# Taking the units of a fused FFT and feed-forward kernel in pairs: two first products, then two second products bank by bank

## The chip, the core and the metric

The kernel runs on one core of a Trainium2 chip. The metric is the device time of one execution in microseconds (us); three executions of the kernel before took 1721.28, 1721.38 and 1722.38 us, the median is 1721.38 us. The core has TensorE (PE, with its weight loads listed apart as PEld), VectorE (DVE), ScalarE (ACT), GpSimd (POOL) and SyncE (SP), which issues the DMAs. Each engine takes its instructions in the order in which they stand in its own list and waits for the others by semaphores.

## What is computed

```python
def _attn_ref(x):                       # x: 8 x 3008 x 256
    X = np.fft.fft(x, axis=1)
    X = np.fft.fft(X, axis=2)
    return X.real.astype(np.float32)

def _moe_ref(x, w_in, w_out):           # x: 24064 x 256, w_in: 256 x 2048, w_out: 2048 x 256
    h = x @ w_in
    g = np.where(h >= 1, h, np.where(h <= -1, 0.0, (h + 1) ** 2 / 4))
    return (g @ w_out).astype(np.float32)

def reference(x, moe_w_in, moe_w_out):
    return _moe_ref(_attn_ref(x).reshape(8 * 3008, 256), moe_w_in, moe_w_out)
```

The real part of a two-dimensional FFT of each of the 8 batches goes through a feed-forward layer of 2048 hidden channels with a smooth step between its two matrix products.

## The kernel before

The FFT of a batch is made by matmuls in 15 pieces: eight pieces of stage 1 (`s1`, L301, copied out by ACT at L322 into `z`), one for the Nyquist row (`ny`, L329, copied out by ACT at L333 as `nyt`), and six of stage 2 (`s2`, L367, split at L186 on ACT and L188 on DVE into a high and a low part, `pqh` and `pql`). The second FFT axis is folded into `w_in`. All these pieces share one PSUM bank, tag `fft`.

The feed-forward part is cut into **units**. A unit is one batch, one of three chunks of its columns (482, 512 and 512 wide) and 128 of the 2048 hidden channels, so there are 8 x 3 x 16 = 384 units, and 16 units in a row add up into the same output. A unit runs through these steps, which the document calls by the short names given here:

- the **first product** (`gemm1`, L418): two PSUM banks, called .0 and .1 here, three matmuls each. The banks come from a ring of three, tag `uv`; a bank is free again when DVE has read it.
- **us** (L433, DVE) reads bank .0; **h0** and **h1** (L441 and L442, DVE) read bank .1 and make the two halves of `h`.
- **relu** (L447, ACT) and **square** (L451, ACT) make `a` from `h`, one after the other on the same tile.
- **larger** (L462, DVE) joins `a` and `h`, both in SBUF.
- **gh** (L466, ACT) rounds `h` to the high part that TensorE multiplies by, and **gl** (L471, POOL, two instructions) forms the rest. Both have rings of four tiles, so the `gh` of a unit takes over the tile of the unit four before it, which must have been multiplied by then. `h` and `a` have rings of three.
- the **second product** (`gemm2`, L572): four PSUM banks `acc0` to `acc3`, three matmuls each (high by high, high by low, low by high), added up over the 16 units of an output. It comes four units later (`LAG`). After the last of the 16 units the four banks are copied out (**evicted**): for all batches but the first, bank 0 by DVE (L559) and banks 1 to 3 by ACT (L557), and two DMAs write them.

The first 48 units or so are written out by hand in a table of steps (`WRITTEN`). Behind it the loop at the end issues unit by unit: first product, activation, the FFT pieces that fall due (`PLAN`), and the second product of the unit four before. The last three units follow a hand-written list (`END`). A scheduler turns the loop's program into the engines' lists: it keeps dependences, but places each instruction by its own estimates, and evictions are given a higher priority (`EVICT_AHEAD`). So the order on ACT and DVE is not the order in the text.

Of the kernel before, what the change touches and what calls it, by code (L numbers as in the profile page):

```python
# [29 lines left out]
NCHUNK = 3  # L30
NFT = FF // P
LAG = 4
EVICT_AHEAD = 150

C_ORDER = [*range(1, 8), 0, *range(8, NC)]
# [87 lines left out]
N_FIXED = 3  # L123
# [5 lines left out]
def fft_ffn_kernel(ctx: ExitStack, tc: tile.TileContext, x, cst, w_in, w_out, out):  # L129
    nc = tc.nc  # L130
# [36 lines left out]
    woh = wts.tile([P, NFT, D], F32R, name="woh")  # L167
    wol = wts.tile([P, NFT, D], F32R, name="wol")
# [211 lines left out]
    def fft_pieces(b):  # L380
        pieces = []
        for q in range(XC):
            pieces.append(stage1(b, q))
        pieces.append(nyquist(b))
        for h in range(NC // 4):
            pieces.append(stage2(b, h))
        return pieces
# [5 lines left out]
    units = []  # L393
    for b in range(NB):
        visits = 1 if b else 2
# [6 lines left out]
    n_units = len(units)  # L402
    acts, outs = {}, {}

    def new_o(i):
        b, k, *_ = units[i]
        return [sb.tile([P, 2, CH], F32, tag="o", name=f"o_{i}_{dh}", bufs=2) for dh in range(2)]

    def gemm1(i):
        b, k, f, *_ = units[i]  # L410
        n = WIDTH[k]
        hi, lo = pq[b, k]
        cols = slice(f * P, (f + 1) * P)
        uv = acts[i] = []
        for m in range(2):
            t = ps.tile([P, CH], F32, tag="uv", name=f"uv_{i}_{m}", bufs=3)
            for j, (w, r) in enumerate(((wh, hi), (wl, hi), (wh, lo))):
                nc.tensor.matmul(t[:, :n], w[m][:, cols], r[:, m, :n], start=(j == 0), stop=(j == 2))  # L418
            uv.append(t[:, :n])
            yield  # L420
# [6 lines left out]
    def common(i):  # L427
        b, k, f, *_ = units[i]
        n = WIDTH[k]
        uv = acts[i]  # L430
        us = sb.tile([P, CH], F32, tag="us", name=f"us_{i}", bufs=2)[:, :n]
        d = delta[:, f : f + 1]
        fixed(i, nc.vector.scalar_tensor_tensor(us, nyb[b, k][:, :n], d, uv[0], op0=ALU.mult, op1=ALU.add), 2)  # L433
        acts[i] = us, uv

    def hidden(i):
        b, k, f, *_ = units[i]
        n = WIDTH[k]
        us, (_, v) = acts[i]
        h = sb.tile([P, 2, CH], F32, tag="h", name=f"h_{i}", bufs=3)[:, :, :n]  # L440
        fixed(i, nc.vector.tensor_tensor(h[:, 0], us, v, op=ALU.subtract), 2)  # L441
        fixed(i, nc.vector.tensor_tensor(h[:, 1], us, v, op=ALU.add), 2)  # L442
        acts[i] = h, sb.tile([P, 2, CH], F32, tag="a", name=f"a_{i}", bufs=3)[:, :, :n]

    def relu(i, sl=slice(0, 2)):
        h, a = acts[i]
        fixed(i, nc.scalar.activation(a[:, sl], h[:, sl], AF.Relu, bias=half, scale=0.5), 2)  # L447

    def square(i, sl=slice(0, 2)):
        _, a = acts[i]  # L450
        fixed(i, nc.scalar.activation(a[:, sl], a[:, sl], AF.Square), 2)  # L451

    def halves(i):
        b, k, *_ = units[i]
        n = WIDTH[k]
        return tuple(
            sb.tile([P, 2, CH], F32R, tag=tag, name=f"{tag}_{i}", bufs=4)[:, :, :n] for tag in ("gh", "gl")
        )

    def larger(i, sl=slice(0, 2)):  # L460
        h, a = acts[i]
        fixed(i, nc.vector.scalar_tensor_tensor(h[:, sl], a[:, sl], 1.0, h[:, sl], op0=ALU.min, op1=ALU.max))  # L462

    def high_half(i, gh, sl=slice(0, 2)):
        h, _ = acts[i]
        fixed(i, nc.scalar.activation(gh[:, sl], h[:, sl], AF.Copy))  # L466

    def low_half(i, gh, gl, sg):
        h, _ = acts[i]
        eng = nc.vector if (i - n_units, sg) in VECTOR_HALVES else nc.gpsimd  # L470
        fixed(i, eng.tensor_tensor(gl[:, sg], h[:, sg], gh[:, sg].bitcast(F32), op=ALU.subtract))  # L471

    def activate(i):
        common(i)
        yield
        hidden(i)
        yield
        relu(i)
        yield
        square(i)  # L480
        yield
        larger(i)
        yield
        gh, gl = halves(i)
        high_half(i, gh)
        yield
        low_half(i, gh, gl, 0)
        yield
        low_half(i, gh, gl, 1)
        acts[i] = gh, gl  # L490

    def finish_units():

        parts = {"a": slice(0, 1), "b": slice(1, 2)}
        g = {}
        for step in END.split():
            kind, at = step[0], step[1]
            i = n_units - N_FIXED + (N_FIXED - 1 if at in parts else int(at))
            sl = parts.get(at, slice(0, 2))
            if kind == "G":  # L500
                drain(gemm1(i))
            elif kind == "M":
                drain(gemm2(i - LAG))
            elif kind == "u":
                common(i)
            elif kind == "h":
                hidden(i)
            elif kind == "r":
                relu(i, sl)
            elif kind == "s":  # L510
                square(i, sl)
            elif kind == "x":
                larger(i, sl)
            else:
                if i not in g:
                    g[i] = halves(i)
                if kind == "g":
                    high_half(i, g[i][0], sl)
                else:
                    low_half(i, *g[i], int(step[2]))  # L520
        acts.update(g)
        for i in range(n_units - LAG, n_units):
            drain(gemm2(i))
# [3 lines left out]
    def drain(step):  # L527
        for _ in step or ():
            pass

    def gemm2(i):
        b, k, f, first, last, (v, visits) = units[i]
        n = WIDTH[k]
        gh, gl = acts.pop(i)
        if first:
            start = -k % 5 if b == NB - 1 else 0
            tags = [BANKS[(start + j) % 5] for j in range(4)]
            accs[:] = [ps.tile([P, CH], F32, tag=t, name=f"acc_{i}_{j}", bufs=1) for j, t in enumerate(tags)]
            if v:

                outs[k] = new_o(i)
                for dh in range(2):
                    nc.sync.dma_start(outs[k][dh][:, :, :n], parts[k][dh, :, :, :n])
        if last:
            o = outs.pop(k) if v else new_o(i)
        banks = [(dh, sg) for dh in range(2) for sg in range(2)]
        if i == n_units - 1:
            banks.sort(key=lambda bank: bank[::-1])

        def evict(dh, sg):  # L550
            acc = accs[dh * 2 + sg]
            dst = o[dh][:, sg, :n]
            with tc.high_priority(offset=EVICT_AHEAD):
                if v:
                    nc.vector.tensor_tensor(dst, acc[:, :n], dst, op=ALU.add)
                elif sg or b and dh:
                    nc.scalar.activation(dst, acc[:, :n], AF.Copy)  # L557
                else:
                    nc.vector.tensor_copy(dst, acc[:, :n])  # L559
            if i == n_units - 1:  # L560
                nc.sync.dma_start(out[b, k, dh, sg, :, :n], dst)
            if sg and v < visits - 1:
                nc.sync.dma_start(parts[k][dh, :, :, :n], o[dh][:, :, :n])
            elif sg and i < n_units - 1:
                nc.sync.dma_start(out[b, k, dh].rearrange("s p t -> p s t")[:, :, :n], o[dh][:, :, :n])

        later = f"M{i}" in written
        for dh, sg in banks:
            wc = slice(dh * P, (dh + 1) * P)
            acc = accs[dh * 2 + sg]  # L570
            for j, (w, g) in enumerate(((woh, gh), (wol, gh), (woh, gl))):
                nc.tensor.matmul(  # L572
                    acc[:, :n], w[:, f, wc], g[:, sg], start=(first and j == 0), stop=(last and j == 2)
                )
            if last and not later:
                evict(dh, sg)
        if last and later:
            for bank in banks:
                yield
                evict(*bank)  # L580
        yield
# [4 lines left out]
    def fill(n):  # L586
# [3 lines left out]
    first = [fft_pieces(b) for b in range(min(NB, 2))]  # L590
# [21 lines left out]
        "G": gemm1,  # L612
        "U": activate,
        "M": gemm2,
    }

# [12 lines left out]
    written = set(WRITTEN.split())  # L629

    plan = {}
# [13 lines left out]
        fill(N_WARM)  # L645
        run_steps(WRITTEN)

    for i in range(n_units - N_FIXED):
        if f"G{i}" not in written:
            drain(gemm1(i))  # L650
            drain(activate(i))
        for f in plan.get(i, ()):
            drain(f if hasattr(f, "send") else f())
        if i >= LAG and f"M{i-LAG}" not in written:
            drain(gemm2(i - LAG))
    finish_units()


# [53 lines left out]
```

## Time and profile before

| | before |
|---|---|
| median of three executions | 1721.38 us |
| span of the profiled execution | 1720.0 us |
| PE busy | 1708.5 us (99%), 7782 matmuls |
| DVE busy | 1384.2 us (80%) |
| ACT busy | 1355.9 us (79%) |
| POOL busy | 1197.4 us (70%) |
| second product, three groups of L572 | 606.5 + 601.8 + 595.3 us |
| first product, three groups of L418 | 305.9 + 301.3 + 298.6 us |

The profiled execution's own time from its first to its last instruction is 1720.0 us, 1.4 us below the median of the three. The busy time of PE counts pipelined matmuls that overlap, so it is read here by the distance from one matmul's start to the next one's. The granted clock of TensorE is full from end to end.

### The profile page before, as it was taken

Reading aid. Unit: us, or ns where it says so; the run is one execution under the profiler, and the core shown is the slowest. Engines: PE = TensorE matmul, PEld = TensorE weight load, DVE = VectorE, ACT = ScalarE, POOL = GpSimd, SP = SyncE. Lnnn points to the kernel's source line nnn. Section 1 sums busy time; section 2 is a strip of 40 time slices with the busy share of each in tenths; the row PEclk is TensorE's granted clock in tenths of the full one; section 3 lists DMA queues with packets and bytes.
Section 4 is the critical chain, followed back from the end, with each engine's and each line's share of the span. In section 5 each row is a group of like instructions: output and inputs, shape, how many; then the busy total and the mean of one; then the engine's idle time right before and its main releaser. Section 6 shows DMA issues by size and latency. Waiting matters only on the chain.

```text
span 1720.0 us, 21494 instructions
## 1 busy us (share of the span) xinstructions
PE 1708.5 (99%) x7782; PEld 1404.1 (82%) x7782; DVE 1384.2 (80%) x1683; ACT 1355.9 (79%) x1593; POOL 1197.4 (70%) x856
## 2 busy tenths in 40 slices
PE   9999999999999999999999999999999999999999
PEld 6878888888888888888888888888788888888776
DVE  6998888777888778887888778887788777888887
ACT  7878877878777877788877887778877788777776
POOL 3777766877667866768666786667766676766775
PEclk9999999999999999999999999999999999999999
DMA  6123320111001010011100111001100001000000
GB/s 234 48 74 119 101 70 25 52 37 53 19 7 60 28 53 25 10 51 38 44 25 10 51 46 35 26 10 60 50 21 26 10 24 43 1 25 24 1 26 25
DMA packets 33456, 72.44 MB, mean 42 GB/s; under 512 B 4547, under 2 KB 9667, under 8 KB 33350
## 3 DMA queue, kind: packets, MB, share of 16 engines
q1 hardware_dynamic: 33350, 71.07, 12.5%
q8 instruction: 61, 1.00, 0.3%
q14 instruction: 45, 0.37, 0.1%
HBM read 43.25 MB, written 27.81 MB: 41 GB/s over the span
## 4 chain that ended last, share of the span: by engine, by line
PE 75%; POOL 11%; issue 5%; ACT 4%; DVE 4%; DMA 0%; SPq 0%; POOLq 0%; ACTq 0%; DVEq 0%
PE acc L572 46%; PE uv L418 23%; POOL gl L471 9%; PE s L367 2%; PE s L301 2%; DVE h L462 2%; ACT gh L466 2%; ACT a L451 1%; POOL y L150 1%; ACT a L447 1%; DVE h L442 1%; DVE h L441 0%; DMA raw<-in_moe_w_in_dram 0%; DVE us L433 0%; PE wps L261 0%
## 5 line engine op out<-in xcount | busy, mean ns | idle before, releaser
L471 POOL TENSOR_TENSOR gl<-h,gh 128x512 fp32r<-128x512 f32 (+1 forms) x764 | 1094.6, 1456 | 487.8 <-ACT gh L466 441.4
L462 DVE SCALAR_TENSOR_TENSOR h<-a,h 128x1024 f32<-128x1024 f32 (+1 forms) x385 | 567.5, 1475 | 237.1 <-ACT a L451 236.6
L466 ACT ACTIVATE gh<-h 128x1024 fp32r<-128x1024 f32 (+1 forms) x385 | 400.6, 1041 | 310.4 <-DVE h L462 272.8
L572 PE MATMUL acc<-gh,woh 128*128 128x512 f32 (+1 forms) x1536 | 606.5, 395 | 0.0
L572 PE MATMUL acc<-gl,woh 128*128 128x512 f32 (+1 forms) x1536 | 601.8, 392 | 0.9 <-POOL gl L471 0.8
L572 PE MATMUL acc<-gh,wol 128*128 128x512 f32 (+1 forms) x1536 | 595.3, 388 | 0.0
L447 ACT ACTIVATE a<-h,half 128x1024 f32<-128x1024 f32 (+1 forms) x385 | 431.8, 1122 | 23.0 <-DVE h L442 20.1
L451 ACT ACTIVATE a<-a 128x1024 f32<-128x1024 f32 (+1 forms) x385 | 399.2, 1037 | 7.8
L572 PEld LDWEIGHTS acc<-gl,woh 128*128 128x128 f32 x1536 | 288.4, 188 | 62.6 <-POOL gl L471 1.9
L572 PEld LDWEIGHTS acc<-gh,wol 128*128 128x128 f32 x1536 | 289.2, 188 | 60.8 <-POOL wol L188 0.4
L572 PEld LDWEIGHTS acc<-gh,woh 128*128 128x128 f32 x1536 | 289.1, 188 | 55.9 <-DVE o L559 0.2
L441 DVE TENSOR_TENSOR h<-us,uv 128x512 f32<-128x512 f32 (+1 forms) x384 | 259.6, 676 | 64.4 <-POOL gl L471 23.6
L418 PE MATMUL uv<-pqh,wh 128*128 128x512 f32 (+1 forms) x768 | 305.9, 398 | 1.1 <-DVE h L442 0.9
L418 PE MATMUL uv<-pql,wh 128*128 128x512 f32 (+1 forms) x768 | 301.3, 392 | 0.0
L418 PE MATMUL uv<-pqh,wl 128*128 128x512 f32 (+1 forms) x768 | 298.6, 389 | 0.0
L433 DVE SCALAR_TENSOR_TENSOR us<-nyb,delta,uv 128x512 f32<-128x512 f32 (+1 forms) x384 | 278.7, 726 | 5.1 <-PE uv L418 4.5
L442 DVE TENSOR_TENSOR h<-us,uv 128x512 f32<-128x512 f32 (+1 forms) x384 | 256.2, 667 | 0.0
L418 PEld LDWEIGHTS uv<-pqh,wh 128*128 128x128 f32 x768 | 144.3, 188 | 38.8 <-DVE h L442 6.8
L418 PEld LDWEIGHTS uv<-pql,wh 128*128 128x128 f32 x768 | 144.3, 188 | 31.9
L418 PEld LDWEIGHTS uv<-pqh,wl 128*128 128x128 f32 x768 | 144.2, 188 | 31.0 <-issue 1.2
L322 ACT ACTIVATE z<-s 64x192 f32<-64x192 f32 x244 | 82.6, 339 | 4.4 <-PE s L301 0.7
L150 POOL TENSOR_TENSOR y<-x 128x384 f32<-128x384 f32 x56 | 80.7, 1443 | 0.7 <-PE s L301 0.7
(59 smaller groups left out, 493.8 us busy)
## 6 DMA issues: line engine op xcount, KB each, us to landing
x<-in_x_dram SPq DMA_DIRECT2D x64, 384.0 KB, 3.1
out_dram<-o SPq DMA_DIRECT2D x30, 512.0 KB, 3.2
out_dram<-o SPq DMA_DIRECT2D x16, 482.0 KB, 3.3
nyb<-nyr SPq DMA_DIRECT2D x23, 256.0 KB, 5.6
raw<-in_moe_w_in_dram SPq DMA_DIRECT2D x8, 512.0 KB, 8.5
raw<-in_moe_w_out_dram SPq DMA_DIRECT2D x8, 512.0 KB, 4.5
part<-o SPq DMA_DIRECT2D x4, 512.0 KB, 2.6
o<-part SPq DMA_DIRECT2D x4, 512.0 KB, 3.5
```

The source lines that it names most:

```text
L150: nc.gpsimd.tensor_tensor(y, t[:, 0], t[:, 1], op=ALU.add)
L322: nc.scalar.activation(dst, src, AF.Copy)
L418: nc.tensor.matmul(t[:, :n], w[m][:, cols], r[:, m, :n], start=(j == 0), stop=(j == 2))
L433: fixed(i, nc.vector.scalar_tensor_tensor(us, nyb[b, k][:, :n], d, uv[0], op0=ALU.mult, op1=ALU.add), 2)
L441: fixed(i, nc.vector.tensor_tensor(h[:, 0], us, v, op=ALU.subtract), 2)
L442: fixed(i, nc.vector.tensor_tensor(h[:, 1], us, v, op=ALU.add), 2)
L447: fixed(i, nc.scalar.activation(a[:, sl], h[:, sl], AF.Relu, bias=half, scale=0.5), 2)
L451: fixed(i, nc.scalar.activation(a[:, sl], a[:, sl], AF.Square), 2)
L462: fixed(i, nc.vector.scalar_tensor_tensor(h[:, sl], a[:, sl], 1.0, h[:, sl], op0=ALU.min, op1=ALU.max))
L466: fixed(i, nc.scalar.activation(gh[:, sl], h[:, sl], AF.Copy))
L471: fixed(i, eng.tensor_tensor(gl[:, sg], h[:, sg], gh[:, sg].bitcast(F32), op=ALU.subtract))
L572: nc.tensor.matmul(acc[:, :n], w[:, f, wc], g[:, sg], start=(first and j == 0), stop=(last and j == 2))
```

## The change

The loop behind the written part steps by two units. It issues the first products and the activations of both, then the FFT pieces due for either, and then the second products of the two units that are four behind, as one call of `gemm2` with a count of two: bank by bank, three matmuls of the one unit and three of the other. Where the pair holds the last of the 16 units, the banks are evicted as before, each after its six matmuls. The last unit of the loop stands alone. Nothing is added or left out: the counts of matmuls, weight loads, DVE, ACT and POOL instructions and DMAs are the same.

```diff
--- before.py
+++ after.py
@@ -30,6 +30,7 @@
 NCHUNK = 3
 NFT = FF // P
 LAG = 4
+PAIRED = 2
 EVICT_AHEAD = 150
 
 C_ORDER = [*range(1, 8), 0, *range(8, NC)]
@@ -528,10 +529,11 @@
         for _ in step or ():
             pass
 
-    def gemm2(i):
-        b, k, f, first, last, (v, visits) = units[i]
+    def gemm2(i, count=1):
+        b, k, _, first, _, (v, visits) = units[i]
+        last = units[i + count - 1][4]
         n = WIDTH[k]
-        gh, gl = acts.pop(i)
+        group = [(units[u][2], *acts.pop(u)) for u in range(i, i + count)]
         if first:
             start = -k % 5 if b == NB - 1 else 0
             tags = [BANKS[(start + j) % 5] for j in range(4)]
@@ -557,21 +559,20 @@
                     nc.scalar.activation(dst, acc[:, :n], AF.Copy)
                 else:
                     nc.vector.tensor_copy(dst, acc[:, :n])
-            if i == n_units - 1:
+            if i + count == n_units:
                 nc.sync.dma_start(out[b, k, dh, sg, :, :n], dst)
             if sg and v < visits - 1:
                 nc.sync.dma_start(parts[k][dh, :, :, :n], o[dh][:, :, :n])
-            elif sg and i < n_units - 1:
+            elif sg and i + count < n_units:
                 nc.sync.dma_start(out[b, k, dh].rearrange("s p t -> p s t")[:, :, :n], o[dh][:, :, :n])
 
         later = f"M{i}" in written
         for dh, sg in banks:
             wc = slice(dh * P, (dh + 1) * P)
             acc = accs[dh * 2 + sg]
-            for j, (w, g) in enumerate(((woh, gh), (wol, gh), (woh, gl))):
-                nc.tensor.matmul(
-                    acc[:, :n], w[:, f, wc], g[:, sg], start=(first and j == 0), stop=(last and j == 2)
-                )
+            terms = [(w[:, f, wc], g[:, sg]) for f, gh, gl in group for w, g in ((woh, gh), (wol, gh), (woh, gl))]
+            for j, (w, g) in enumerate(terms):
+                nc.tensor.matmul(acc[:, :n], w, g, start=(first and j == 0), stop=(last and j == len(terms) - 1))
             if last and not later:
                 evict(dh, sg)
         if last and later:
@@ -645,14 +646,19 @@
         fill(N_WARM)
         run_steps(WRITTEN)
 
-    for i in range(n_units - N_FIXED):
-        if f"G{i}" not in written:
-            drain(gemm1(i))
-            drain(activate(i))
-        for f in plan.get(i, ()):
-            drain(f if hasattr(f, "send") else f())
+    i = 0
+    while i < n_units - N_FIXED:
+        group = range(i, min(i + PAIRED, n_units - N_FIXED))
+        for u in group:
+            if f"G{u}" not in written:
+                drain(gemm1(u))
+                drain(activate(u))
+        for u in group:
+            for f in plan.get(u, ()):
+                drain(f if hasattr(f, "send") else f())
         if i >= LAG and f"M{i-LAG}" not in written:
-            drain(gemm2(i - LAG))
+            drain(gemm2(i - LAG, len(group)))
+        i = group.stop
     finish_units()
```

The numbers in the names below are those of units (`uv_212_0` is bank .0 of unit 212's first product, `gh_208` the high part of unit 208, `acc_208_0` bank 0 of the output that unit 208 begins, `o_206_0` and `o_207_0` its predecessor's eviction). Line numbers of the changed kernel are one higher up to L471 and two or three higher behind.

TensorE at units 212 and 213, before:

```order
L418 MATMUL uv_212_0_8504<-pqh_4_1_7754,wh0_69 128x512
L418 MATMUL uv_212_0_8504<-pqh_4_1_7754,wl0_71 128x512
L418 MATMUL uv_212_0_8504<-pql_4_1_7755,wh0_69 128x512
L418 MATMUL uv_212_1_8508<-pqh_4_1_7754,wh1_70 128x512
L418 MATMUL uv_212_1_8508<-pqh_4_1_7754,wl1_72 128x512
L418 MATMUL uv_212_1_8508<-pql_4_1_7755,wh1_70 128x512
L301 MATMUL s1_5_2_8528<-cs_66,y_5_2_8404 128x144
L301 MATMUL s1_5_2_8528<-cs_66,y_5_2_8404 128x192
L301 MATMUL s1_5_2_8528<-cs_66,y_5_2_8404 128x144
L572 MATMUL acc_208_0_8538<-gh_208_8365,woh_73 128x512
L572 MATMUL acc_208_0_8538<-gh_208_8365,wol_74 128x512
L572 MATMUL acc_208_0_8538<-gl_208_8366,woh_73 128x512
```

and now:

```order
L419 MATMUL uv_212_0_8504<-pqh_4_1_7776,wh0_69 128x512
L419 MATMUL uv_212_0_8504<-pqh_4_1_7776,wl0_71 128x512
L419 MATMUL uv_212_0_8504<-pql_4_1_7777,wh0_69 128x512
L419 MATMUL uv_212_1_8508<-pqh_4_1_7776,wh1_70 128x512
L419 MATMUL uv_212_1_8508<-pqh_4_1_7776,wl1_72 128x512
L419 MATMUL uv_212_1_8508<-pql_4_1_7777,wh1_70 128x512
L419 MATMUL uv_213_0_8526<-pqh_4_1_7776,wh0_69 128x512
L419 MATMUL uv_213_0_8526<-pqh_4_1_7776,wl0_71 128x512
L419 MATMUL uv_213_0_8526<-pql_4_1_7777,wh0_69 128x512
L419 MATMUL uv_213_1_8530<-pqh_4_1_7776,wh1_70 128x512
L419 MATMUL uv_213_1_8530<-pqh_4_1_7776,wl1_72 128x512
L419 MATMUL uv_213_1_8530<-pql_4_1_7777,wh1_70 128x512
```

The second product of units 208 and 209 stood between the two first products (and has moved behind both); the second of the pair now follows the first at once. Bank 0 of the second product, now:

```order
L575 MATMUL acc_208_0_8560<-gh_208_8365,woh_73 128x512
L575 MATMUL acc_208_0_8560<-gh_208_8365,wol_74 128x512
L575 MATMUL acc_208_0_8560<-gl_208_8366,woh_73 128x512
L575 MATMUL acc_208_0_8560<-gh_209_8387,woh_73 128x512
L575 MATMUL acc_208_0_8560<-gh_209_8387,wol_74 128x512
L575 MATMUL acc_208_0_8560<-gl_209_8388,woh_73 128x512
L575 MATMUL acc_208_1_8561<-gh_208_8365,woh_73 128x512
```

Two units' matmuls go to a bank before the next bank begins.

ScalarE where the output of units 192 to 207 is evicted, before:

```order
L447 ACTIVATE a_210_8441<-h_210_8438,half_76 128x1024
L451 ACTIVATE a_210_8441<-a_210_8441 128x1024
L557 ACTIVATE o_207_0_8484<-acc_192_1_7915 128x482
L557 ACTIVATE o_207_1_8485<-acc_192_2_7916 128x482
L557 ACTIVATE o_207_1_8485<-acc_192_3_7917 128x482
L466 ACTIVATE gh_210_8445<-h_210_8438 128x1024
L447 ACTIVATE a_211_8475<-h_211_8472,half_76 128x1024
L322 ACTIVATE z_5_8288<-s1_5_2_8528 64x24x8
L451 ACTIVATE a_211_8475<-a_211_8475 128x1024
L447 ACTIVATE a_212_8517<-h_212_8514,half_76 128x1024
L322 ACTIVATE z_5_8288<-s1_5_2_8528 64x24x8
L451 ACTIVATE a_212_8517<-a_212_8517 128x1024
```

and now:

```order
L448 ACTIVATE a_210_8441<-h_210_8438,half_76 128x1024
L452 ACTIVATE a_210_8441<-a_210_8441 128x1024
L559 ACTIVATE o_206_0_8472<-acc_192_1_7937 128x482
L448 ACTIVATE a_211_8463<-h_211_8460,half_76 128x1024
L559 ACTIVATE o_206_1_8473<-acc_192_2_7938 128x482
L467 ACTIVATE gh_210_8445<-h_210_8438 128x1024
L559 ACTIVATE o_206_1_8473<-acc_192_3_7939 128x482
L452 ACTIVATE a_211_8463<-a_211_8463 128x1024
L467 ACTIVATE gh_211_8467<-h_211_8460 128x1024
L448 ACTIVATE a_212_8517<-h_212_8514,half_76 128x1024
```

The three evictions stood in a row behind the square of unit 210; now they stand apart, and the `gh` of 210 and the eviction of the last bank stand ahead of the square of 211, whose `gh` in turn stands ahead of the relu of 212.

VectorE at the same place, before:

```order
L433 SCALAR_TENSOR_TENSOR us_212_8512<-nyb_4_1_7280,delta_75,uv_212_0_8504 128x512
L441 TENSOR_TENSOR h_212_8514<-us_212_8512,uv_212_1_8508 128x512
L442 TENSOR_TENSOR h_212_8514<-us_212_8512,uv_212_1_8508 128x512
L462 SCALAR_TENSOR_TENSOR h_211_8472<-a_211_8475,h_211_8472 128x1024
L433 SCALAR_TENSOR_TENSOR us_213_8562<-nyb_4_1_7280,delta_75,uv_213_0_8554 128x512
L462 SCALAR_TENSOR_TENSOR h_212_8514<-a_212_8517,h_212_8514 128x1024
L441 TENSOR_TENSOR h_213_8564<-us_213_8562,uv_213_1_8558 128x512
L442 TENSOR_TENSOR h_213_8564<-us_213_8562,uv_213_1_8558 128x512
L433 SCALAR_TENSOR_TENSOR us_214_8596<-nyb_4_1_7280,delta_75,uv_214_0_8588 128x512
L441 TENSOR_TENSOR h_214_8598<-us_214_8596,uv_214_1_8592 128x512
L462 SCALAR_TENSOR_TENSOR h_213_8564<-a_213_8567,h_213_8564 128x1024
```

and now:

```order
L434 SCALAR_TENSOR_TENSOR us_212_8512<-nyb_4_1_7268,delta_75,uv_212_0_8504 128x512
L442 TENSOR_TENSOR h_212_8514<-us_212_8512,uv_212_1_8508 128x512
L463 SCALAR_TENSOR_TENSOR h_211_8460<-a_211_8463,h_211_8460 128x1024
L443 TENSOR_TENSOR h_212_8514<-us_212_8512,uv_212_1_8508 128x512
L434 SCALAR_TENSOR_TENSOR us_213_8534<-nyb_4_1_7268,delta_75,uv_213_0_8526 128x512
L442 TENSOR_TENSOR h_213_8536<-us_213_8534,uv_213_1_8530 128x512
L443 TENSOR_TENSOR h_213_8536<-us_213_8534,uv_213_1_8530 128x512
L463 SCALAR_TENSOR_TENSOR h_212_8514<-a_212_8517,h_212_8514 128x1024
L463 SCALAR_TENSOR_TENSOR h_213_8536<-a_213_8539,h_213_8536 128x1024
L434 SCALAR_TENSOR_TENSOR us_214_8596<-nyb_4_1_7268,delta_75,uv_214_0_8588 128x512
L442 TENSOR_TENSOR h_214_8598<-us_214_8596,uv_214_1_8592 128x512
```

The two larger steps of a pair (212 and 213) now stand behind all six reads of `uv`, and the `us` of the next pair behind both of them; the larger of 211 has moved ahead of h1 of 212, where it stood behind it.

## Rows read from the trace of the kernel before

**Rows 1.** Windows: stretch, PE, PEld, DVE, ACT, POOL busy (count), clock, DMA share, GB/s

```profile
310.00:1690.00 1380.00, 1378.85 (x6292) 1140.82 (x6291) 1102.37 (x1322) 1086.45 (x1249) 972.58 (x682) 1.00 0.10 31
```

**Rows 2.** Waits of TensorE, 310 to 1690 us: us in total, times, longest

```profile
PEld uv L418 <- DVE us L433: 2.6, 9, 0.5
PEld uv L418 <- DVE h L442: 2.0, 8, 0.3
...
PEld s L367 <- ACT nyt L333: 1.9, 3, 1.1
...
PE s L367 <- ACT nyt L333: 0.8, 2, 0.7
```

**Rows 3.** Timeline of TensorE from 1001.5 us: start, duration, engine, line, operation, tiles

```profile
1001.60 0.40 PE L418 MATMUL uv<-pqh,wh 128*128 128x512 f32 x1
...
1002.06 0.40 PE L418 MATMUL uv<-pql,wh 128*128 128x512 f32 x1
...
1003.00 0.39 PE L572 MATMUL acc<-gh,woh 128*128 128x512 f32 x1
1003.23 0.39 PE L572 MATMUL acc<-gh,wol 128*128 128x512 f32 x1
1003.46 0.40 PE L572 MATMUL acc<-gl,woh 128*128 128x512 f32 x1
1003.69 0.39 PE L572 MATMUL acc<-gh,woh 128*128 128x512 f32 x1
...
1005.77 0.40 PE L418 MATMUL uv<-pqh,wh 128*128 128x512 f32 x1
...
1007.16 0.98 PE L301 MATMUL s<-cs,y 128*128 128x144 f32 x6
1007.88 0.49 PE L572 MATMUL acc<-gh,woh 128*128 128x512 f32 x1
1008.21 0.39 PE L572 MATMUL acc<-gh,wol 128*128 128x512 f32 x1
```

**Rows 4.** Timeline of VectorE from 1002 us

```profile
1002.38 1.23 DVE L462 SCALAR_TENSOR_TENSOR h<-a,h 128x1024 f32<-128x1024 f32 x1 [1.24 <-ACT a L451]
...
1004.12 0.74 DVE L433 SCALAR_TENSOR_TENSOR us<-nyb,delta,uv 128x512 f32<-128x512 f32 x1
1004.99 0.69 DVE L441 TENSOR_TENSOR h<-us,uv 128x512 f32<-128x512 f32 x1
1005.60 0.68 DVE L442 TENSOR_TENSOR h<-us,uv 128x512 f32<-128x512 f32 x1
1006.95 1.55 DVE L462 SCALAR_TENSOR_TENSOR h<-a,h 128x1024 f32<-128x1024 f32 x1 [0.67 <-ACT a L451]
1008.43 0.73 DVE L433 SCALAR_TENSOR_TENSOR us<-nyb,delta,uv 128x512 f32<-128x512 f32 x1
```

**Rows 5.** Timeline of ScalarE from 1002 us

```profile
1003.72 1.06 ACT L466 ACTIVATE gh<-h 128x1024 fp32r<-128x1024 f32 x1 [1.37 <-DVE h L462]
1004.69 1.14 ACT L447 ACTIVATE a<-h,half 128x1024 f32<-128x1024 f32 x1
1005.86 1.06 ACT L451 ACTIVATE a<-a 128x1024 f32<-128x1024 f32 x1
1006.82 1.14 ACT L447 ACTIVATE a<-h,half 128x1024 f32<-128x1024 f32 x1
```

**Rows 6.** Timeline of VectorE at 340 us: a larger that meets a gl

```profile
339.71 2.34 DVE L462 SCALAR_TENSOR_TENSOR h<-a,h 128x1024 f32<-128x1024 f32 x1 [0.53 <-ACT a L451]
```

**Rows 7.** Timeline of GpSimd at the same place

```profile
338.42 2.55 POOL L471 TENSOR_TENSOR gl<-h,gh 128x512 fp32r<-128x512 f32 x2
```

**Rows 8.** Timeline of ScalarE: three evictions in a row, at 958 us

```profile
957.96 1.50 ACT L557 ACTIVATE o<-acc 128x482 f32<-128x482 f32 x3
```

**Rows 9.** Groups by form, ScalarE, 310 to 1690 us: count, busy us, mean ns, idle before

```profile
L322 ACT ACTIVATE z<-s 64x192 f32<-64x192 f32 x188 | 63.7, 339 | 2.6
...
L186 ACT ACTIVATE pqh<-s 128x512 fp32r<-128x512 f32 x36 | 20.9, 580 | 0.0
```

## The prediction

> **What bounds the kernel now.** I read first the busy time of the engines in the stretch behind the written part [rows 1]: PE is busy in 1378.85 of 1380 us at the full clock, and no other engine comes near that. Then the waits of PE there [rows 2]: the first products wait 4.6 us in all for DVE to free a `uv` bank, and stage 2 waits 2.7 us for the copy of the Nyquist row. Last its timeline [rows 3]: a unit of 18 matmuls takes from 1001.60 to 1005.77, 4.17 us, so 0.232 us for a matmul and 8.34 us for a pair. So TensorE sets the time, its matmuls stay as many, and the change can win only where PE waits or where a step from matmul to matmul becomes shorter. It can lose wherever PE comes to wait.
>
> **What the order can win.** A pair's second products change banks eight times before and four times now. From 1003.23 to 1003.46 a step stays in its bank, from 1003.46 to 1003.69 it changes it, and both take 0.23 us [rows 3]; the rows show hundredths, so a change of bank costs between nothing and 0.01 us. Four fewer in each of 165 paired products: 0 to 6.6 us. I take 3, the middle, since nothing is nearer to an end.
>
> In the Trainium skill, "TensorE: Matmul & The Clock Gate", section "Back-to-back issue gap", the distance of warm matmuls follows from the columns alone, 215.7 ns measured at 512. A bank plays no part in it, so by that page this gain is nil; the trace has 232 ns and leaves up to 10 open.
>
> The waits for the Nyquist copy, 2.7 us, may go, since a whole pair now lies between the piece and its successor: 0 to 2.7, I take 1.5.
>
> **A plain pair.** Now the second first product follows the first at once, and its bank .1 takes the ring's third place behind the bank .0 of the same pair. It must wait until DVE's us of the pair's first unit has read that bank. I set the start of a pair's first matmul to 0. PE wants that bank at 9 x 0.232 = 2.09. The third matmul starts at 0.46 and lasts 0.40 [rows 3], so us starts at 0.90 (0.04 for the semaphore, an estimate) and lasts 0.74 [rows 4]; with 0.28 for the semaphore and the weight load ahead of the matmul (an estimate from one matmul step of 0.23) it could go on at 1.92. That fits by 0.17, if DVE is free at 0.90.
>
> DVE is free when the larger of the unit before is done. Its chain, from us at 0.90: h0 0.87 after us, h1 0.61 after that, 0.68 long [rows 4], so the first relu starts at 3.09; square 1.17 after relu and the next relu 0.96 after square, as in the row of 1004.69, 1005.86 and 1006.82 [rows 5]: relu of the second unit at 5.22, its square at 6.39 to 7.45, its larger at 7.48. A larger is 1.23 long, or 1.55 beside POOL, and us follows some 0.08 ahead of its end (1006.95 to 1008.43) [rows 4]: DVE is free at 8.63 to 8.95. The next pair needs it at 8.34 + 0.90 = 9.24. So a plain pair fits, with 0.29 to 0.61 to spare and 0.17 more on PE. The gh of a pair waits for matmuls that are over 0.7 before the pair's end, and gl has 2.55 us for its two instructions [rows 7] before h0 of the second unit needs its tile at 3.8; both fit. A piece of stage 1 lengthens the pair's time on PE by 0.81 (1007.16, 1007.88 and 1008.21 against two steps of 0.232 less [rows 3]) and puts two copies of 0.34 into the chain; a piece of stage 2 (eight matmuls to six) puts 0.58 into it [rows 9]. Those fit as well.
>
> **The pair behind an eviction** is what costs. In ACT's new list the gh of 210 and the eviction of bank 3 stand ahead of the square of 211, and the gh of 211 stands ahead of the relu of 212. I set 0 to the end of the second product of 206 and 207, the first matmul of 212. Bank 2 is complete at -1.15 (six matmuls from the end, each 0.22 at 482 columns), its eviction takes 0.5 [rows 8], and gh of 210 runs from -0.3 to 0.76. Bank 3's eviction follows to 1.3, and the square of 211, ready since long, runs only from 1.25 to 2.3. Its larger can begin at 2.46, behind h0 of 212, and then meets a gl: that of 210 runs in two halves to 3.4. Where a larger starts in the middle of a gl it takes 2.34 [rows 6] while gl keeps its 2.55 [rows 7], so it waits for the instruction to end: larger to 4.5, gh of 211 from 4.6, relu of 212 0.96 later at 5.55 instead of 3.09. From there the plain chain: square 6.7, relu of 213 7.7, its square 8.85, its larger 9.95, us of 214 at 11.1 to 11.4, done at 11.8 to 12.2, and bank .1 of 215 at 12.1 to 12.4 instead of 8.34 + 2.09 = 10.43. PE waits 1.65 to 2.0 us. With a piece in the pair PE wants the bank 0.8 later and the chain is 0.1 to 0.7 longer, as far as its copies slip between relu and square, so the wait is 1.1 to 1.9. I take 1.5. The next pair starts 1.5 us later on PE and is plain again: the wait isn't made up, but doesn't grow.
>
> The new list has this order at all outputs that end behind the written part, save the last: units 63, 79 and so on to 367, 20 places. 20 x 1.5 = 30 us, from 20 x 1.1 = 22 to 20 x 2.0 = 40. Before, the square of 210 came first, the three evictions in a row took 1.50 [rows 8], and the next bank of the ring had a second product's 2.77 us (1003.00 to 1005.77 [rows 3]) of room.
>
> What hides such a wait elsewhere is work that may overtake. The same page of the Trainium skill, "TensorE: Matmul & The Clock Gate" (section "Step-by-step: what each phase is for"), says that PE draws only weight loads ahead and keeps its matmuls in program order. By that the second products behind the waiting matmul stand still, and the 30 us remain; could they overtake, it would be nil. No row here shows it either way.
>
> **The ends.** Where the loop begins, evictions by DVE (about 0.7 each) come ahead of the larger of 48 and 49 with PE short of work: 0 to 4, I take 2. Ten pairs at the two ends have both us ahead of h0, which puts 0.74 [rows 4] into a chain with 0.46 to 0.78 to spare: 0 to 0.28 each, 0 to 2.8, I take 1. DMAs are as many as before and not late in any of these chains.
>
> **Sum**, on the profiled 1720.0: 30 - 3 - 1.5 + 2 + 1 = +28.5. Beside the median of 1721.38 that is 1749.9, so 1750. Its own bounds: 22 - 6.6 - 2.7 = +12.7, and 40 + 4 + 2.8 = +46.8: 1734 to 1768.
>
> **Rivals.** (1) Every pair waits. If the larger of each second unit met a gl or a fold, it would take 2.34 instead of 1.23 [rows 4, 6], 1.11 more than the 0.78 at most that a pair has to spare: some 0.33 in each of 145 other pairs, 48 us more, 1798. Against it: POOL's two gl start some 0.4 after the pair's start and are over at 0.4 + 2 x 2.55 = 5.5 [rows 7], before 7.48. (2) The evictions don't bite, because gh and square get through before the pair begins: what stays is -3 - 1.5 + 2 + 1, 1720. For it: before, the same evictions cost PE nothing. (3) The other sign: with no wait at the evictions and the dearest change of bank, -6.6 - 2.7, the time is 1712. This decides if a bank change costs a hundredth of a microsecond and the places cost under 0.4 us each. That the change does not do what it says is out: the new list has six matmuls in a row to a bank.
>
> **The numbers.** About 0.2%, 3.4 us, is what a measurement of this kernel can tell from no change. My forecast 0.73, rival 1 0.12, rival 2 0.09, rival 3 0.06. All of the first two is slower: 0.85; same 0.09; faster 0.06. The range goes down to rival 2 and up to the nearer half of rival 1, 1720 to 1785; rival 3, half of each of the other two, 0.16 in all, stay out.
>
> **What would show it.** In the trace after, waits of the first product for us (DVE) of 1 to 2 us, 20 times, each in the pair behind an eviction, and 20 to 40 us in sum; none in plain pairs; matmul steps of 0.23 us as before; the clock full. I am wrong if those waits are spread over all pairs (rival 1) or absent (rivals 2 and 3), or if the steps in a bank of six get shorter than 0.22 us, which I hold to be excluded.

## The result and the profile after

The changed kernel takes 1735.23 us (median of 4 runs, 1734.76 to 1735.52) beside 1721.33 for the kernel before (4 runs, 1720.95 to 1722.38): a ratio of 1.0076 with an interval of 1.0064 to 1.0088, or 13.9 us more. The forecast was 28.5 more. The profiled execution has a span of 1733.3 us, 13.3 more than that of before.

The page of the changed kernel, its parts 1, 2 and 5:

```profile
span 1733.3 us, 21764 instructions
...
PE 1712.5 (99%) x7782; PEld 1406.3 (81%) x7782; DVE 1351.1 (78%) x1683; ACT 1357.3 (78%) x1593; POOL 1082.6 (62%) x856
...
PEclk9999999999999999999999999999999999999999
...
L472 POOL TENSOR_TENSOR gl<-h,gh 128x512 fp32r<-128x512 f32 (+1 forms) x764 | 974.2, 1305 | 596.7 <-ACT gh L467 568.4
L463 DVE SCALAR_TENSOR_TENSOR h<-a,h 128x1024 f32<-128x1024 f32 (+1 forms) x385 | 524.5, 1364 | 172.8 <-ACT a L452 172.3
...
L419 PE MATMUL uv<-pqh,wh 128*128 128x512 f32 (+1 forms) x768 | 306.3, 399 | 11.1 <-DVE us L434 9.2
```

As many matmuls, the clock full throughout, and VectorE and GpSimd less busy (1384.2 and 1197.4 us before). The last row has the loss: the first matmul of a first product's bank waits for us. Across the stretch behind the written part, where before showed TensorE busy in all but a microsecond [rows 1], it now misses ten:

```profile
310.00:1690.00 1380.00, 1370.21 (x6244) 1132.89 (x6243) 1062.77 (x1312) 1080.92 (x1246) 856.40 (x677) 1.00 0.09 31
```

What it waits for there, as weight loads (PEld) and as matmuls (PE): total, times, longest. The wait for the Nyquist row's copy [rows 2] is gone, and the one for us has grown from 2.6 to 19.2. A load that waits has also lost the 0.23 us by which it else leads its matmul, so these totals overstate what TensorE lost. The loss is therefore read from the starts of the matmuls.

```profile
PEld uv L419 <- DVE us L434: 19.2, 22, 2.2
...
PE uv L419 <- DVE us L434: 8.9, 15, 1.7
```

The timeline of TensorE shows where. Five of the places, each named by its first matmul of bank .1 of the pair's second unit (units 71, 87, 103, 119 and 215; at 103 a matmul of the second product stands ahead of it in the list):

```profile
340.77 0.40 PE L419 MATMUL uv<-pql,wh 128*128 128x512 f32 x1
342.91 0.50 PE L419 MATMUL uv<-pqh,wh 128*128 128x512 f32 x1 [1.75 <-DVE us L434]
...
415.79 0.50 PE L419 MATMUL uv<-pqh,wh 128*128 128x512 f32 x1 [0.41 <-DVE us L434]
...
484.57 0.38 PE L575 MATMUL acc<-gh,woh 128*128 128x482 f32 x1
485.10 0.48 PE L419 MATMUL uv<-pqh,wh 128*128 128x482 f32 x1
485.42 0.39 PE L419 MATMUL uv<-pqh,wl 128*128 128x482 f32 x1
...
554.63 0.50 PE L419 MATMUL uv<-pqh,wh 128*128 128x512 f32 x1 [0.69 <-DVE us L434]
...
977.01 0.40 PE L419 MATMUL uv<-pql,wh 128*128 128x512 f32 x1
978.10 0.50 PE L419 MATMUL uv<-pqh,wh 128*128 128x512 f32 x1 [0.69 <-DVE us L434]
978.44 0.40 PE L419 MATMUL uv<-pqh,wl 128*128 128x512 f32 x1
```

At unit 215 the step is 1.09 us (977.01 to 978.10) where 0.23 is the rule: 0.86 lost. The step behind it, 978.10 to 978.44, is 0.10 longer as well, so the place costs 0.96. Read so, from the start of one matmul to the start of the next, the 20 places come to:

| units with the waiting bank | places | lost in each, us | sum, us |
|---|---|---|---|
| 71 | 1 | 2.0 | 2.0 |
| 119, 167, 215, 263, 311 (512 columns, a piece of stage 1) | 5 | 0.96 | 4.8 |
| 87, 135, and so on to 327 (512 columns, a piece of stage 2) | 6 | 0.69 | 4.1 |
| 103, 151, and so on to 343 (482 columns, a piece of stage 2) | 6 | 0.40 | 2.4 |
| 359 (512 columns) | 1 | 0.67 | 0.7 |
| 375 | 1 | 0 | 0 |

14.0 us in all, 0.70 a place. No other first product between units 72 and 360 waits by more than 0.1 us. Three of the 22 waits stand outside the table, near the two ends: 0.27 us lost at unit 65, 0.78 at 365 and 0.59 at 377. The place at 375 is empty because the order is another there: the relu of 372 starts 3.11 us after its pair does and the gh of 371 only at 5.71, behind it, and the larger of 371 stands behind h1 of 372. So the order stands at 19 outputs, not at the 20 that the prediction counted; at the last one the wait comes a pair later, at 377.

The whole difference is laid out by when a unit's first matmul starts, after against before: 0.46 later at unit 48, where the pairs begin (nothing of the program differs ahead of it; other kernels below stood between 0.15 earlier and 0.93 later there); 2.53 at unit 64; 4.83 at 72; 7.88 at 152; 11.51 at 248; 13.47 at 344; 14.16 at 360; and 13.27 at the last matmul.

**One place, followed through.** ScalarE, VectorE and GpSimd around the first matmul of unit 212, at 965.99 (zero of the prediction's reckoning). ScalarE of the changed kernel:

```profile
965.06 0.56 ACT L559 ACTIVATE o<-acc 128x482 f32<-128x482 f32 x1
965.51 1.06 ACT L467 ACTIVATE gh<-h 128x1024 fp32r<-128x1024 f32 x1
966.46 0.57 ACT L559 ACTIVATE o<-acc 128x482 f32<-128x482 f32 x1
966.91 1.07 ACT L452 ACTIVATE a<-a 128x1024 f32<-128x1024 f32 x1
970.38 1.06 ACT L467 ACTIVATE gh<-h 128x1024 fp32r<-128x1024 f32 x1 [2.40 <-DVE h L463]
971.34 1.14 ACT L448 ACTIVATE a<-h,half 128x1024 f32<-128x1024 f32 x1
972.39 0.32 ACT L323 ACTIVATE z<-s 64x192 f32<-64x192 f32 x1
972.60 1.04 ACT L452 ACTIVATE a<-a 128x1024 f32<-128x1024 f32 x1
973.54 1.14 ACT L448 ACTIVATE a<-h,half 128x1024 f32<-128x1024 f32 x1
974.71 0.34 ACT L323 ACTIVATE z<-s 64x192 f32<-64x192 f32 x1
975.07 1.06 ACT L452 ACTIVATE a<-a 128x1024 f32<-128x1024 f32 x1
```

VectorE:

```profile
968.38 1.91 DVE L463 SCALAR_TENSOR_TENSOR h<-a,h 128x1024 f32<-128x1024 f32 x1
970.21 0.67 DVE L443 TENSOR_TENSOR h<-us,uv 128x512 f32<-128x512 f32 x1
...
973.67 1.48 DVE L463 SCALAR_TENSOR_TENSOR h<-a,h 128x1024 f32<-128x1024 f32 x1 [0.72 <-ACT a L452]
976.16 1.23 DVE L463 SCALAR_TENSOR_TENSOR h<-a,h 128x1024 f32<-128x1024 f32 x1 [1.01 <-ACT a L452]
977.30 0.74 DVE L434 SCALAR_TENSOR_TENSOR us<-nyb,delta,uv 128x512 f32<-128x512 f32 x1
```

and GpSimd:

```profile
966.65 2.56 POOL L472 TENSOR_TENSOR gl<-h,gh 128x512 fp32r<-128x512 f32 x2 [2.61 <-ACT gh L467]
...
971.52 2.56 POOL L472 TENSOR_TENSOR gl<-h,gh 128x512 fp32r<-128x512 f32 x2 [0.34 <-ACT gh L467]
```

The square of unit 211 (966.91) stands behind an eviction and a gh. Its larger (968.38) meets the gl of 210 and takes 1.91. ScalarE then stands still for 2.40 us, since the next thing in its list is the gh of 211, which needs that larger; the relu of 212 follows at 971.34, 5.35 after zero. From there the plain chain runs, larger of 213 at 976.16, us of 214 at 977.30 to 978.04, and bank .1 of 215 at 978.10. This is the chain of the prediction, link for link.

One link more stands in VectorE's list, and the prediction doesn't name it: the larger of 211 also stands ahead of h1 of 212, which therefore starts only at 970.21. The relu of 212 needs that h1 as well. So it waits for the larger of 211 by two ways: by VectorE's order until 970.88, where h1 ends, and by ScalarE's order until 971.34, where the gh makes room. Without the gh ahead of it the relu could have come some 0.4 earlier (an estimate from these two rows), not the whole 2.26 that lie between 5.35 and the prediction's 3.09. Both orders stand in plain pairs as well and cost nothing there: in the pair of unit 220 the larger of 219 is over at 0.39 us and the relu of 220 starts at 3.10, behind its h1. They cost only where the square, and with it the larger, is late.

### The profile page after: what moved, and what is told of

Same layout as the page of the kernel before. It is cut to its first block, busy times and chain, and to the rows that moved or that the text cites. A ratio compares the mean times of both kernels' runs of the same rounds, so it can differ in the third digit from the quotient of the medians.

```text
span 1733.3 us, 21764 instructions
## 1 busy us (share of the span) xinstructions
PE 1712.5 (99%) x7782; PEld 1406.3 (81%) x7782; DVE 1351.1 (78%) x1683; ACT 1357.3 (78%) x1593; POOL 1082.6 (62%) x856
## 4 chain that ended last, share of the span: by engine, by line
PE 73%; DVE 9%; ACT 8%; POOL 5%; issue 4%; DMA 0%; SPq 0%; DVEq 0%; POOLq 0%; ACTq 0%
PE acc L575 46%; PE uv L419 22%; DVE h L463 5%; POOL gl L472 4%; ACT a L452 3%; ACT a L448 3%; PE s L302 2%; DVE us L434 2%; ACT gh L467 2%; PE s L368 2%; DVE h L442 1%; POOL y L151 1%; DVE h L443 1%; DMA raw<-in_moe_w_in_dram 0%; ACT pqh L187 0%
## 5 line engine op out<-in xcount | busy, mean ns | idle before, releaser
L472 POOL TENSOR_TENSOR gl<-h,gh 128x512 fp32r<-128x512 f32 (+1 forms) x764 | 974.2, 1305 | 596.7 <-ACT gh L467 568.4
L463 DVE SCALAR_TENSOR_TENSOR h<-a,h 128x1024 f32<-128x1024 f32 (+1 forms) x385 | 524.5, 1364 | 172.8 <-ACT a L452 172.3
L467 ACT ACTIVATE gh<-h 128x1024 fp32r<-128x1024 f32 (+1 forms) x385 | 393.0, 1037 | 118.9 <-DVE h L463 88.8
L419 PE MATMUL uv<-pqh,wh 128*128 128x512 f32 (+1 forms) x768 | 306.3, 399 | 11.1 <-DVE us L434 9.2
L151 POOL TENSOR_TENSOR y<-x 128x384 f32<-128x384 f32 x56 | 86.2, 1542 | 3.9 <-PE s L302 3.9
```

Of the source, the lines that this page charges most:

```text
L151: nc.gpsimd.tensor_tensor(y, t[:, 0], t[:, 1], op=ALU.add)
```

## Experiments

The theory: the loss is the order of ScalarE's list at an eviction, which makes the next relu wait for a late larger. The rivals: it is ScalarE's time for the evictions; it comes from pairs as such, wherever they stand; or six matmuls to a bank cost or gain something by themselves.

**Two ways to take the square of the second unit out from behind the eviction and the gh.** In the first kernel the evictions are due later, by one number, and the square of 211 comes ahead of the gh of 210:

```diff
-EVICT_AHEAD = 150
+EVICT_AHEAD = 0
```

> The changed kernel with EVICT_AHEAD 0 instead of 150, nothing else: on ScalarE the square of the second unit then stands ahead of the gh of the first and of the last eviction. Theory A (the 13.9 us are the waits at the 20 evictions, some 12 us, and some 3 us at the two ends, less the 2.7 us of the Nyquist waits): the 20 waits go, the time is 1719 to 1724 us. Theory B (taking first products in pairs costs as such, and the places are only where it shows): the waits come up elsewhere, the time stays at 1730 us or above.

In the second the first products stay in pairs, and the second products go unit by unit again, three matmuls to a bank:

```diff
-            drain(gemm2(i - LAG, len(group)))
+            for u in group:
+                drain(gemm2(u - LAG))
```

> The changed kernel, with the first products still in pairs, but the second products unit by unit, three matmuls to a bank. Theory A: the scheduler then puts the three evictions behind the square of the second unit, so no wait at the 20 places: 1719 to 1724 us. Theory B (pairs of first products cost as such): 1730 us or above.

Measured: 1719.43 us (11 runs, ratio to before 0.9984, 0.9975 to 0.9993) and 1719.08 (11 runs, 0.9979, 0.9970 to 0.9988). Both lie where the theory had them. The waits at the places are gone in both. What is left behind unit 64 stands at no place: a step of 0.40 us at unit 65, and one of 1.03 at unit 69 (1.05 in the second). ScalarE of the first at the same place, and what TensorE waits for from 310 to 1690 us:

```profile
956.27 1.14 ACT L448 ACTIVATE a<-h,half 128x1024 f32<-128x1024 f32 x1
957.43 0.57 ACT L559 ACTIVATE o<-acc 128x482 f32<-128x482 f32 x1
957.90 1.05 ACT L452 ACTIVATE a<-a 128x1024 f32<-128x1024 f32 x1
958.85 1.05 ACT L467 ACTIVATE gh<-h 128x1024 fp32r<-128x1024 f32 x1
959.79 0.57 ACT L559 ACTIVATE o<-acc 128x482 f32<-128x482 f32 x1
960.32 1.06 ACT L467 ACTIVATE gh<-h 128x1024 fp32r<-128x1024 f32 x1
961.28 0.56 ACT L559 ACTIVATE o<-acc 128x482 f32<-128x482 f32 x1
962.32 1.15 ACT L448 ACTIVATE a<-h,half 128x1024 f32<-128x1024 f32 x1 [0.48 <-DVE h L443]
```

```profile
PE uv L419 <- DVE us L434: 0.6, 1, 0.6
```

The three evictions are all there and as long. Unit 212 starts at 959.07 in this trace, so its relu starts at 3.25 instead of 5.35, and waits for VectorE's h1, not for the gh. The first matmul of 215's bank .1 comes 11.26 after zero, where it came 12.11 after. This pair of kernels also gives the price of a place without any reckoning on single steps: from unit 104 on, the changed kernel falls behind the one with late evictions by 2.1 us every 48 units (2.68 at unit 104, 4.79, 6.92, 9.04, 11.15, 13.27 at 344), three places each, so 0.71 a place.

The kernel with late evictions alone doesn't show the cause, since the number does more than turn this order, as the last experiment shows. The second kernel leaves the number as it was.

**The evictions' time, without their order, and their order changed by more of them.** Bank 3, the last, copied out twice:

```diff
                     nc.scalar.activation(dst, acc[:, :n], AF.Copy)
+                    if dh and sg:
+                        nc.scalar.activation(dst, acc[:, :n], AF.Copy)
```

> The changed kernel with bank 3 copied out twice, the second time onto the same place: 20 more ScalarE copies of 0.58 us. The order stays, and the second copy stands between the square of the second unit and its gh, where ScalarE waits for the larger on VectorE. Theory A (the chain square, larger, gh, relu sets the wait): the copy lies in that wait, so 1734 to 1737 us as before. The rival (ScalarE's load at the evictions sets it): 20 x 0.5 us more, 1744 us or above.

Bank 2 copied out twice (the same with `if dh and not sg`), which moves the gh of the second unit behind the relu of the next pair:

> The changed kernel with bank 2 copied out twice: as much added work, but the scheduler now puts the gh of the second unit behind the relu of the next pair instead of ahead of it, so that this relu starts at about 3.1 us into the pair instead of 5.3. Theory A (the order gh ahead of relu sets the wait): most of the 20 waits go although ScalarE has more to do, 1723 to 1728 us. The rival (the load at the evictions): 1744 us or above.

Measured: 1736.60 (4 runs, 1735.47 to 1737.30, ratio 1.0084, 1.0071 to 1.0098) and 1723.07 (11 runs, 1.0005, 0.9996 to 1.0014), both where the theory had them. With bank 3 twice, 24 more copies and 14.3 us more of ScalarE's time, the wait from 310 to 1690 us is what it was without:

```profile
PE uv L419 <- DVE us L434: 8.9, 15, 1.7
```

With bank 2 twice ScalarE runs

```profile
959.63 1.06 ACT L467 ACTIVATE gh<-h 128x1024 fp32r<-128x1024 f32 x1
960.58 0.58 ACT L561 ACTIVATE o<-acc 128x482 f32<-128x482 f32 x1
961.03 0.59 ACT L559 ACTIVATE o<-acc 128x482 f32<-128x482 f32 x1
961.48 1.08 ACT L452 ACTIVATE a<-a 128x1024 f32<-128x1024 f32 x1
963.20 1.15 ACT L448 ACTIVATE a<-h,half 128x1024 f32<-128x1024 f32 x1 [0.65 <-DVE h L443]
...
964.50 1.06 ACT L467 ACTIVATE gh<-h 128x1024 fp32r<-128x1024 f32 x1
```

VectorE

```profile
962.49 0.68 DVE L443 TENSOR_TENSOR h<-us,uv 128x512 f32<-128x512 f32 x1
963.09 1.32 DVE L463 SCALAR_TENSOR_TENSOR h<-a,h 128x1024 f32<-128x1024 f32 x1
```

and the bank .1 of 215 comes on time: 971.36, again 11.26 after the start of unit 212 (960.10). (L561 is the second copy of bank 2.) So 21 more copies, some 9 us of ScalarE's time, make the kernel 12 us faster. The evictions' time is not what costs. Here the square is still late (961.48, 1.38 after zero); it was enough that the relu of 212 no longer waits for the larger of 211. Both orders that held it have turned: on ScalarE the second gh has slipped behind the relu, and on VectorE that larger has slipped behind h1 of 212. No run turns one of the two without the other, so how the 14 us divide between them is not shown. Of the 19 waits 18 are gone; unit 71 keeps one of 1.3 us. Either end of the chain undoes the wait.

**Fewer pairs.** Pairs only between units 64 and 351:

```diff
-        group = range(i, min(i + PAIRED, n_units - N_FIXED))
+        group = range(i, i + (PAIRED if 64 <= i < 352 else 1))
```

> The changed kernel with pairs only from unit 64 to unit 351; units before and behind come singly, and 17 of the 20 evictions keep the new order. Theory A, with the waits read from the changed kernel's trace (0.58 us at six places, 0.29 at six, 0.85 at five, so 9.5 us, and the 2.7 us of the Nyquist waits saved, from 1721.4): 1727 to 1730 us, some 6 us below the changed kernel, because the ends (3 us) and the three dearest or irregular places (2.5 us) are gone. The rival (every pair costs a little, 13.9 us over 166 pairs): 144 pairs of them remain, 12 us, 1733 to 1735 us.

Measured: 1731.47 (5 runs, 1.0055, 1.0041 to 1.0069), between the two expectations. The places from unit 87 on have the steps of the full change (0.82, 0.53 and 1.09 at units 87, 103 and 119, and so on to 343). What neither theory had is the passage from single units to pairs: bank .1 of unit 67 waits 1.33 us and bank .0 of 65 waits 0.46, in return for the start that was saved. So this run confirms the places, and says little on the ends.

**Six to a bank, first products apart.** Second products of two units share their banks, and the first products stand between banks 1 and 2 and behind bank 3, as in single order:

```diff
+            if count == 2 and (dh, sg) == (0, 1):
+                yield
...
+        second = gemm2(i - LAG, len(group)) if i >= LAG and f"M{i-LAG}" not in written else None
         for u in group:
...
-        for u in group:
             for f in plan.get(u, ()):
                 drain(f if hasattr(f, "send") else f())
+            if second:
+                next(second, None)
+        drain(second)
```

> The changed kernel with six matmuls to a bank, but the first products not side by side: the first of a pair, then banks 0 and 1 of the paired second product, the second of the pair, then banks 2 and 3. Theory A (a change of bank costs TensorE nothing): the steps stay at 0.231 us and the time is that of the kernel before within 2 us, 1719 to 1723 us. The rival (a change of bank costs up to 0.01 us): 165 x 4 x 0.01 = 6.6 us less, down to 1715 us.

Measured: 1717.02 (5 runs, 0.9968, 0.9956 to 0.9981), 5 us under the kernel before and the fastest of all. The time lies below what the theory had and within what the rival had, so the steps have to decide. The mean step from one matmul of the second product to the next is 229.7 ns over the whole run, 229.8 before, 229.8 after and 229.7 in each of the two kernels of the first experiment, with three or six to a bank alike. Inside the changed kernel, at 512 columns, a step within a bank from one unit's terms to the other's is 232.8 ns and one to the next bank 233.4; over the 660 changes that the edit saves, that is 0.4 us at most. So the gain is not one of the matmuls. As far as the trace shows it comes from waits: those of TensorE's loads in the stretch have shrunk from 4.6 for a `uv` bank [rows 2] to 0.6, and none for the Nyquist copy is left. From the first matmul of unit 64 to that of 360 the steps into and within FFT pieces take 2.7 us less than before, and from 360 to 383 the steps within first products 2.0 less.

```profile
PEld ny L330 <- ACT a L448: 1.5, 4, 0.4
PEld uv L419 <- DVE us L434: 0.6, 1, 0.6
```

**Late evictions without pairs**, the kernel before with the same one number changed to 0:

> The kernel before with EVICT_AHEAD 0 instead of 150, to see what that number does without pairs. Both theories: units stand alone, the evictions have a second product's time of room either way, so 1720 to 1723 us. If it moved by more than 3 us, the gain of the same edit in the paired kernel would not be that of the order at the evictions alone.

Measured: 1726.51 (10 runs, 1.0023, 1.0014 to 1.0032), 4 us slower, where both theories had it at 1720 to 1723. Among its waits, the largest of TensorE's:

```profile
PEld acc L572 <- ACT o L557: 8.5, 18, 0.9
```

A new wait: the second product for the eviction of its own bank. Unit by unit, a bank is wanted again sooner than with a pair's two first products in between, so late evictions hurt here and not in pairs, where TensorE has no such wait from 310 to 1690 us. The number that cures the pairs is not better as such. It moved by more than the 3 us that had been set as a limit, so by that expectation the gain of late evictions in pairs can't be put down to the order at the evictions alone. That reading rests on the kernel with second products unit by unit and on bank 2 copied twice, which leave the number as it was.

## Why the prediction was right and wrong

**Right: the mechanism and its places.** It said that waits of the first product for us would stand in the pairs behind evictions, 20 of them, and none in plain pairs. 19 of the 20 are there, behind the outputs named, and at unit 212 the chain ran in the order worked out. Undoing the order took them away in three ways, but for one at unit 71 in one of them. Three more waits do stand in other pairs, all near the ends. What the prediction left out is that VectorE's order holds the relu as well.

**Wrong: the size of the eviction term.** It was put at 20 x 1.5 = 30 us, at least 20 x 1.1; it is 14.0, or 0.70 a place. This is the step that failed. A place's wait is a small difference of two long sums, and its parts were off in one direction. For the place of unit 212, which has a piece of stage 1 in the pair and for which 1.1 to 1.9 was worked out:

- TensorE wants the bank at 10.43 and 0.8: forecast 11.23, measured 977.01 + 0.23 = 977.24, 11.25 after zero. Right. (The prediction takes two steps off to reach the 0.8; one goes off, 1.05 - 0.23.)
- The relu of 212 was put at 5.55 and came at 5.35: larger of 211 ended at 4.30, not 4.5 (it took 1.91 where the row chosen [rows 6] has 2.34, since the gl ended sooner), and the gh began at 4.39.
- us of 214 was put at 11.1 to 11.4 and the piece's 0.1 to 0.7 on top, 11.65 in the middle; it came at 11.31. The piece's copies cost the chain 0.4, the middle, but the larger of 213 was the short one, 1.23 with GpSimd idle, not the middle of 1.23 and 1.55.
- Behind us 0.28 was put for the semaphore and the weight load. The matmul starts 0.06 after us ends (978.04 to 978.10), and the next step is 0.10 longer: 0.16.

The middle of the working was 11.65 + 0.74 + 0.28 - 11.23 = 1.44, taken as 1.5. 0.34 from the chain, 0.12 from the tail and 0.02 from the first line turn 1.44 into 0.96, which was measured. The rest of the difference is that one place stood for all 20. A pair with a piece of stage 2 wants its bank 0.1 later and its chain was 0.2 shorter (us of 86 at 11.13), so 0.69; and six places lie in the 482-column range, where larger takes 1.26 us in the mean of the stretch instead of 1.38 and everything else is shorter too, so 0.40. Only unit 71, where a larger took 2.26, reached the price that was taken for all. And at one place of the 20, at 375, the list doesn't have the order, and there is no wait.

**The other terms.**

| term | forecast, us | measured, us | from |
|---|---|---|---|
| pairs behind evictions | +30 | +14.0 | the table of places |
| bank changes saved | -3 | 0 | steps of 229.8 ns before and after |
| Nyquist and other waits gone | -1.5 | -2.4 | units 64 to 360: 11.6 later, less 14.0 |
| start, units 48 to 64 | +2 | +2.1 | 0.46 later, then 2.53 |
| last pairs, from 360 | +1 | -0.9 | 14.16 later, then 13.27 |
| the part ahead of the pairs | 0 | +0.5 | not changed by the edit |

They sum to 13.3. The third row is what is left over of a difference, and the fourth and fifth are differences of starts. The fewer-pairs kernel, single up to unit 64, loses none of the 2.1 there. The 3 us for the bank changes were taken as the middle of what rounded rows left open; the mean over thousands of steps says nothing is there. The Trainium skill's page "TensorE: Matmul & The Clock Gate" gives two figures for the step at 512 columns: the 215.7 ns that the prediction quotes, which stand in section "Step-by-step: what each phase is for", and about 131 ns for a stream of weight loads and matmuls in section "Back-to-back issue gap". The steps here fit neither: they are 230 to 234 ns at 512 columns, and the trace decides. The same page's rule on order (section "Step-by-step: what each phase is for"), that matmuls stay in program order, agrees with the trace: between 977.01 and 978.10 no matmul of the second product of 210 and 211 ran, though the last of its operands, the gl of 211, was done at 974.08. The 1 us for the last pairs was wrong in sign. Two waits did come in those pairs, 0.78 us at unit 365, behind pairs with both us ahead of h0, and 0.59 at 377, a pair behind the last eviction; but the single order had waits of its own in the same stretch, which the sum left out, and they went: from unit 360 to 383 the matmuls take 97.58 us, and took 97.98 before.

**The rivals.** Rival 1 (every pair waits) is out: but for the three at the ends, plain pairs don't wait, and VectorE waits for TensorE at a us 126 times in the stretch. Rivals 2 and 3 (evictions don't bite) are out for this kernel, but rival 2 is what the two repaired kernels show: 1719, near the 1720 that it gave. Rival 3 also needed a price on a change of bank, and there is none.

## What to carry to other kernels

Where a change regroups work on one engine, read in what order the in-order queues of the other engines get theirs: here a relu that stood behind the larger of the unit before, in ScalarE's list by a gh and in VectorE's by h1, cost 14 us, and the same work in another order cost nothing. When a wait is worked out as the difference of two chains, take each duration from the row of that width and that neighbourhood and add no reserve at each link, since a few tenths too much, 0.46 here, are half of what was measured; and work it out for every kind of place, not for one, after looking whether each place has the order at all. A mean over all steps of the trace settles a hundredth of a microsecond that rounded rows leave open.

## What the runs showed of the hardware

- A matmul held up by a bank starts 0.06 us after the read that frees it has ended, and the next follows 0.34 after instead of 0.23; seen at all the places at 512 columns. The record of its weight load stands at the same 978.10, where other loads stand 0.23 ahead of their matmul:

```profile
978.10 0.19 PEld L419 LDWEIGHTS uv<-pqh,wh 128*128 128x128 f32 x1 [1.13 <-DVE us L434]
```

- VectorE's larger (two inputs in SBUF) takes 1.23 us where GpSimd is idle when it starts, and 1.91 (unit 211) and 2.26 (unit 67) where it starts in the middle of a gl; the one at 968.38 ended 1.08 after the gl did (966.65 and 2.56). The Trainium skill, "SBUF — State Buffer", section "🔬 SBUF: two separate sides", has the ports that the two engines share as a lock held for a whole instruction, and the rows fit that. The changed order also meets less of it: gl went from 1456 to 1305 ns in the mean and larger from 1475 to 1364, over 150 us of the two engines' time that bought nothing, since neither sets the end.
- Neighbours on ScalarE overlap: behind instructions of 1.06 and 0.57 us the next starts after 0.95 and 0.45 (965.51, 966.46, 966.91).
